# Second product of a feed-forward kernel: column halves of TensorE take two blocks of 512 tokens instead of two halves of one block's tokens, for the last 64 outputs

## The chip, the cores and the metric

The program runs on one core of one Trainium2 chip. The metric is the device time of one execution in microseconds. Times inside an execution come from a profiled run, and count from its first instruction.

## What is computed

A causal convolution with 7 taps, whose weights are a softmax made for each token and head, is followed by a feed-forward layer with a squared ReLU. There are 32,768 tokens of 192 numbers, and 2,048 hidden units.

```python
w = exp(weight_gen - max(weight_gen, -1)); w = w / (sum(w, -1) + 1e-9)   # 8 heads, 7 taps
x = einsum('bshk,bskhg->bshg', w, x_unf)       # x_unf: the last 7 tokens, 24 channels a head
h = x @ w_in                                   # 192 -> 2048
g = maximum(h, 0) ** 2
out = g @ w_out                                # 2048 -> 192
```

## The kernel before

**Tiling.** Each of the 128 partitions owns 256 consecutive tokens. A chunk is 4 tokens of every partition, 512 tokens; there are `NCH` = 64 chunks. VectorE makes the convolution of a later chunk (multiplies, line 344, and adds, line 349), the transposed result goes through DRAM and back (lines 525, 531, 536), and ScalarE and VectorE split it into a high and a low half-precision part (lines 392, 398). Every second chunk, the odd ones, also loads two chunks of input (`load_group`, lines 110 and 111) and works out their scales (`size_steps`, `descale`: line 138 on ScalarE, six small instructions on VectorE).

**Batches.** A chunk has 4 batches (b = 0 to 3) of two pairs j of feed-forward blocks. A block is 128 hidden units. In each batch TensorE does the first product of its own two pairs (`mm1`, line 565) and then the second product of the two pairs of the batch before (`mm2`), so the second product of a chunk's last batch falls into batch 0 of the next chunk. Meanwhile ScalarE takes each pair out of PSUM with `relu` (line 572), squares it (`square`, 576) and rounds it to half precision (`high`, 580); VectorE subtracts to get the remainder (`low`, 584). The order on every engine is the order in which the program is written, with `late` putting the `low`s of a batch into the next batch, after its first product, and `todo` the pieces of convolution behind them.

**TensorE in quarters.** The array works as four tiles of 64 rows by 64 columns. The row halves take the two halves of a block's 128 hidden units and write their sums to two PSUM banks; the column halves write to the lower and the upper 64 partitions. Products are made three times: high by high, high by low weights, low by high.

**The second product, transposed.** For chunks 4 to 62 (`turned(c)`, 59 chunks) outputs lie on partitions and tokens on columns. The first accumulator, `accs[c][0]`, takes outputs 0 to 127 (column halves: 0 to 63 and 64 to 127) with 512 tokens in each of two banks. The second, `accs[c][1]`, takes outputs 128 to 191; there the column halves are given two halves of 256 tokens each (line 617). There is one buffer of each accumulator.

**Taking it out.** In batch 1 of the next chunk, after that batch's first product is issued, `finish` copies one bank of each accumulator to SBUF with ScalarE (line 679) and adds the other bank with VectorE (line 680), 512 columns for the first and 256 for the second accumulator. The second product of the new chunk, which is next on TensorE, needs both accumulators free. Then `store_turned` scales the sums (line 702), transposes them (line 703) and issues 24 output DMAs on SyncE's queue (line 710).

Of the kernel before, what the change touches and what calls it, by code (L numbers as in the profile page):

```python
# [8 lines left out]
F32 = mybir.dt.float32  # L9
# [4 lines left out]
ALU = mybir.AluOpType  # L14
# [15 lines left out]
def kernel(  # L30
# [9 lines left out]
    nc = tc.nc  # L40
    B, S, D = x.shape
# [3 lines left out]
    P = 128  # L45
# [4 lines left out]
    TC = 4  # L50
    NCH = n_chunks or R // TC
# [3 lines left out]
    D1 = 64  # L55
    ND = D // D1
    N = TC * P
    NJ = NF // 2
# [12 lines left out]
    op = ctx.enter_context(tc.tile_pool(name="op", bufs=2))  # L71
# [13 lines left out]
    V = const.tile([P, NF, 3 * D], F16, name="V")  # L85
# [6 lines left out]
    act, ts, tt = nc.scalar.activation, nc.vector.tensor_scalar, nc.vector.tensor_tensor  # L92
# [69 lines left out]
    def descale(gi):  # L162
        row = att.tile([P, Q], F32, name="f", bufs=3)
        f = falls[gi] = row[:, 0:1]
        d = downs.pop(gi)
        dq = d.broadcast_to([P, Q])
        stt(out=row, in0=dq, scalar=back, in1=dq, op0=ALU.mult, op1=ALU.mult)
        if turned(gi * CPG):
            spread_falls[gi] = to_all(row)
# [23 lines left out]
    def block(j, i):  # L193
        return 4 * (j // 2) + 2 * i + j % 2
# [105 lines left out]
    HALVES = slice(0, D1), slice(D1, P)  # L300
# [240 lines left out]
    phs, rgs, ghs, gls, accs = {}, {}, {}, {}, {}  # L541

    def turned(c):
        return TURNED <= c < NCH - 1
# [33 lines left out]
    def high(c, j):  # L578
        gh = ghs[c, j] = gp.tile([P, 2, N], F16, name="gh")
        act(gh, rgs[c, j], AF.Copy, scale=1.0 / LIFT)  # L580
# [5 lines left out]
    def new_accs(c):  # L586
        accs[c] = [ps_o.tile([P, 2, N], F32, name=f"acc{i}") for i in range(2 if c else 1)]
# [14 lines left out]
    def mm2_turned(c, j):  # L602
        if j == 0:
            new_accs(c)
        gh, gl = ghs.pop((c, j)), gls.pop((c, j))
        for i in range(2):
            fb = block(j, i)
            for n, g in enumerate((gh, gh, gl)):
                fl = dict(start=fb == 0 and n == 0, stop=fb == NF - 1 and n == 2)
                for col in HALVES:  # L610
                    for r, rows in enumerate(HALVES):
                        d = n * D + col.start
                        nc.tensor.matmul(accs[c][0][col, r], V[rows, fb, d:d + D1], g[rows, i], **fl)  # L613
                for m, col in enumerate(HALVES):
                    for r, rows in enumerate(HALVES):
                        d = n * D + P
                        nc.tensor.matmul(  # L617
                            accs[c][1][col, r, 0:N // 2], V[rows, fb, d:d + D1],
                            g[rows, i, m * N // 2:(m + 1) * N // 2], **fl,
                        )  # L620

    ends = {}

# [40 lines left out]
    outs, sums_t = {}, {}  # L664

    def finish(c, p):
        if c == 0:
            if p == 0:
                outs[c] = op.tile([P, TC, D], F32, name="o_sb")
            nc.scalar.copy(outs[c][:, 2 * p:2 * p + 2], accs[c][0][:, :, p * D:(p + 1) * D])  # L670
            return
        acc = accs[c][p]
        if turned(c):
            if p == 0:
                sums_t[c] = op.tile([P, TC * D], F32, name="s", bufs=1)
            n0, n1 = ((0, N), (N, N + N // 2))[p]
            n = n1 - n0
            tmp = op.tile([P, N], F32, name="tmp")
            nc.scalar.copy(tmp[:, 0:n], acc[:, 1, 0:n])
            tt(out=sums_t[c][:, n0:n1], in0=acc[:, 0, 0:n], in1=tmp[:, 0:n], op=ALU.add)  # L680
            return
        if p == 0:
            outs[c] = op.tile([P, TC, D], F32, name="o_sb")
        o = outs[c][:, 2 * p:2 * p + 2]
        f = falls[c // CPG]
        o = o.rearrange("p t d -> p (t d)")
        tmp = op.tile([P, N], F32, name="tmp")
        n = 2 * D
        act(tmp[:, 0:n], acc[:, 1, 0:n], AF.Copy, scale=f)
        stt(out=o, in0=acc[:, 0, 0:n], scalar=f, in1=tmp[:, 0:n], op0=ALU.mult, op1=ALU.add)  # L690

    def finish_last(c):
        o = outs[c]
        for t in range(TC):
            stt(out=o[:, t], in0=ends[t], scalar=falls[c // CPG], in1=o[:, t], op0=ALU.mult, op1=ALU.add)
            nc.sync.dma_start(out=out_v[:, c * TC + t, :], in_=o[:, t])

    def store_turned(c):
        o = op.tile([P, TC * D], F32, name="o_sb")
        sm = sums_t.pop(c)  # L700
        sb = sm.rearrange("p (t n) -> p t n", n=P)
        tt(out=sb, in0=sb, in1=spread_falls[c // CPG].broadcast_to(sb.shape), op=ALU.mult)
        nc.vector.transpose(o, sm)  # L703
        for col in range(0, D, Q):
            for t in range(TC):
                if col < P:
                    p0, n0 = col, t * P
                else:
                    p0, n0 = 2 * t // TC * D1 + col - P, N + t % 2 * P
                nc.sync.dma_start(  # L710
                    out=out_v[:, c * TC + t, col:col + Q].rearrange("(q i) j -> i q j", i=Q),
                    in_=o[p0:p0 + Q, n0:n0 + P].rearrange("i (q j) -> i q j", j=Q),
                )

    def store(c):
        nc.sync.dma_start(out=out_v[:, c * TC:(c + 1) * TC, :], in_=outs[c])
# [112 lines left out]
    for p in range(2):  # L829
        finish(0, p)  # L830
# [14 lines left out]
    def at(c, b, f):  # L845
        todo.setdefault((c + b // NB, b % NB), []).append(f)
# [41 lines left out]
    for c in range(1, NCH + 1):  # L888
        for b in range(NB if c < NCH else 2):
            js = (2 * b, 2 * b + 1)  # L890
            if c < NCH:
                if b == 0 and c % 2 and (c + 3) // 2 * CPG < NCH:
                    load_group((c + 3) // 2)
                if c % 2 and b == 2 and (c + 3) // 2 * CPG < NCH:
                    total, scales = size_steps((c + 3) // 2)
                    b1 = 5 if c == 1 else 2
                    at(c, b1, total)
                    b2 = 6 if c == 1 else 3
                    at(c, b2, scales)
                    at(c, b2, lambda gi=(c + 3) // 2: descale(gi))  # L900
                if b == 0 and c + 2 < NCH and c + 2 > 2:
                    plan_conv(c + 2)
                for j in js:
                    mm1(c, j)
            early = b == 1 and 2 <= c <= TURNED
            if early:
                for p in range(2):
                    finish(c - 1, p)
            run(late)
            late.clear()  # L910
            if c == NCH and b == 1:
                finish_last(c - 1)
            elif b == (0 if c == NCH else 1) and c > 1:
                for p in range(0 if early else 2):
                    finish(c - 1, p)
                if turned(c - 1):
                    store_turned(c - 1)
                elif c < NCH:
                    store(c - 1)
            turn = turns.pop(c + 1, None) if b == NB - 1 else None  # L920
            if b == NB - 1 and c + 1 in splits and turn is None:
                for f in splits.pop(c + 1):
                    f()
            if pend and turn is None:
                mm2(*pend.pop(0))
            elif pend:
                one = pend.pop(0)
                mm2(*one, slice(0, 3))
                turn[0]()
                mm2(*one, slice(3, 4))  # L930
                turn[1]()
                mm2(*one, slice(4, 8))
            if c < NCH:
                relu(c, js[0])
                square(c, js[0])
                relu(c, js[1])
                high(c, js[0])
                sp = splits.pop(c + 1) if turn is not None else []
                run(sp[:1])
                square(c, js[1])  # L940
                run(sp[1:3])
                high(c, js[1])
                pend.append((c, b))
                late += [lambda c=c, j=js[0]: low(c, j)] + between.pop((c, b), [])
                late += [lambda c=c, j=js[1]: low(c, j)] + behind.pop((c, b), [])
                fs = todo.pop((c, b), [])
                if sp:
                    run(fs[:2])
                    run(sp[3:4])
                    run(fs[2:4])  # L950
                    run(sp[4:])
                    run(fs[4:])
                else:
                    run(fs)
# [30 lines left out]
```

## Time and profile before

| | us |
|---|---|
| median of 3 runs | 2036.22 |
| lowest, highest | 2035.5, 2037.34 |
| the profiled execution, first to last instruction (span) | 2033.1 |
| median less span | 3.1 |
| TensorE busy | 2024.1 (100%) |
| VectorE busy | 1864.3 (92%) |
| ScalarE busy | 1747.0 (86%) |

The profile gives the span of the execution, not its time with what lies around it; the difference to the median of the runs stands in the table in its place. In the rows PE is TensorE, PEld its weight loads, DVE is VectorE, ACT ScalarE, SPq SyncE's queue. A busy matmul engine is one that has a matmul in flight; four matmuls on four tiles run at once.

### The profile page before, as it was taken

Reading aid. Unit: us, or ns where it says so; the run is one execution under the profiler, and the core shown is the slowest. Engines: PE = TensorE matmul, PEld = TensorE weight load, DVE = VectorE, ACT = ScalarE, POOL = GpSimd, SP = SyncE. Lnnn points to the kernel's source line nnn. Section 1 sums busy time; section 2 is a strip of 40 time slices with the busy share of each in tenths; the row PEclk is TensorE's granted clock in tenths of the full one; section 3 lists DMA queues with packets and bytes.
Section 4 is the critical chain, followed back from the end, with each engine's and each line's share of the span. In section 5 each row is a group of like instructions: output and inputs, shape, how many; then the busy total and the mean of one; then the engine's idle time right before and its main releaser. Section 6 shows DMA issues by size and latency. Waiting matters only on the chain.

```text
span 2033.1 us, 92340 instructions
## 1 busy us (share of the span) xinstructions
PE 2024.1 (100%) x42124; PEld 1473.8 (72%) x42124; DVE 1864.3 (92%) x2457; ACT 1747.0 (86%) x2011; POOL 13.7 (1%) x18
## 2 busy tenths in 40 slices
PE   9999999999999999999999999999999999999999
PEld 8777777777777777777777777777777777777776
DVE  8999999999999999999999999999999999999984
ACT  6988888888888888888888888888888888888887
POOL 2000000000000000000000000000000000000000
PEclk9999999999999999999999999999999999999999
DMA  6233333332332333333323333333233233333321
GB/s 189 64 97 91 74 65 76 89 94 74 66 89 73 96 82 84 62 78 89 93 73 65 90 75 94 84 71 74 73 95 92 72 65 82 82 96 77 59 60 23
DMA packets 303552, 164.02 MB, mean 81 GB/s; under 512 B 215360, under 2 KB 273728, under 8 KB 299192
## 3 DMA queue, kind: packets, MB, share of 16 engines
q1 hardware_dynamic: 303160, 158.11, 32.0%
q8 instruction: 329, 5.39, 1.1%
q14 instruction: 63, 0.52, 0.1%
HBM read 108.43 MB, written 49.56 MB: 78 GB/s over the span
## 4 chain that ended last, share of the span: by engine, by line
PE 95%; DVE 3%; DMA 1%; ACT 0%; issue 0%; SPq 0%; POOL 0%; DVEq 0%
PE ph L565 47%; PE acc L613 30%; PE acc L617 15%; PE acc L658 1%; PE acc L597 1%; DVE pr L344 1%; DVE pr L349 1%; DVE gl L584 1%; DMA xT<-xd 0%; DMA xl<-xd 0%; DMA xd<-xr 0%; DMA wt<-in_weight_gen_dram 0%; DVE o_sb L690 0%; PE ph L633 0%; DMA xt<-in_x_dram 0%
## 5 line engine op out<-in xcount | busy, mean ns | idle before, releaser
L565 PEld LDWEIGHTS <-W 64*64 64x64 f16 (+1 forms) x17568 | 634.8, 107 | 319.5 <-issue 4.1
L565 PE MATMUL ph<-xh,W 64*64 64x512 f16 (+1 forms) x11712 | 754.6, 376 | 0.0
L572 ACT ACTIVATE g<-ph 128x1024 f32<-128x1024 f32 x504 | 512.0, 1016 | 239.4 <-PE ph L565 239.4
L584 DVE SCALAR_TENSOR_TENSOR gl<-gh,g 128x1024 f16<-128x1024 f16 x504 | 609.3, 1220 | 110.1 <-ACT gh L580 99.3
L613 PE MATMUL acc<-gh,V 64*64 64x512 f16 x7552 | 696.3, 376 | 0.0
L617 PE MATMUL acc<-gh,V 64*64 64x256 f16 x7552 | 576.9, 269 | 0.1
L613 PEld LDWEIGHTS <-V 64*64 64x64 f16 x11328 | 406.8, 107 | 205.6 <-issue 1.1
L576 ACT ACTIVATE g<-g 128x1024 f32<-128x1024 f32 x512 | 538.8, 1052 | 8.0
L580 ACT ACTIVATE gh<-g 128x1024 f16<-128x1024 f32 x504 | 530.2, 1052 | 8.0
L565 PE MATMUL ph<-xl,W 64*64 64x512 f16 (+1 forms) x5856 | 428.7, 376 | 1.5 <-DMA xl<-xd 1.1
L617 PEld LDWEIGHTS <-V 64*64 64x64 f16 x11328 | 406.7, 107 | 17.2 <-issue 0.3
L344 DVE TENSOR_TENSOR pr<-xt,wt 128x768 f32<-128x768 f32 x434 | 408.1, 953 | 2.1
L613 PE MATMUL acc<-gl,V 64*64 64x512 f16 x3776 | 389.4, 376 | 0.5 <-DVE gl L584 0.5
L349 DVE TENSOR_TENSOR pr<-pr 128x768 f32<-128x768 f32 x376 | 358.8, 954 | 2.2
L617 PE MATMUL acc<-gl,V 64*64 64x256 f16 x3776 | 288.4, 269 | 0.0
L398 DVE TENSOR_TENSOR xl<-xT,xh 128x512 f16<-128x512 f32 x180 | 113.6, 686 | 21.3 <-ACT xh L392 19.8
L392 ACT CAST xh<-xT 128x512 f16<-128x512 f32 x180 | 98.5, 610 | 0.9 <-DMA xT<-xd 0.9
L658 PE MATMUL acc<-V,gh 64*128 64x192 f16 x960 | 62.6, 243 | 0.0
L658 PE MATMUL acc<-V,gl 64*128 64x192 f16 x480 | 60.8, 243 | 0.1
L525 DVE STREAM_TRANSPOSE xr<-pr 128x768 f32<-128x768 f32 x60 | 58.7, 979 | 2.1
L680 DVE TENSOR_TENSOR s<-acc,tmp 128x512 f32<-128x512 f32 x118 | 59.9, 550 | 0.0
L703 DVE STREAM_TRANSPOSE o_sb<-s 128x768 f32<-128x768 f32 x59 | 57.7, 978 | 2.1
(99 smaller groups left out, 680.5 us busy)
## 6 DMA issues: line engine op xcount, KB each, us to landing
xT<-xd SPq DMA_DIRECT2D x120, 384.0 KB
xt<-in_x_dram SPq DMA_DIRECT2D x31, 1344.0 KB
xd<-xr SPq DMA_DIRECT2D x240, 96.0 KB
out_dram<-o_sb SPq DMA_DIRECT2D x1416, 16.0 KB
wt<-in_weight_gen_dram SPq DMA_DIRECT2D x31, 224.0 KB
raw<-in_moe_w_in_dram SPq DMA_DIRECT2D x8, 384.0 KB
raw<-in_moe_w_out_dram SPq DMA_DIRECT2D x4, 768.0 KB
fd<-ft SPq DMA_DIRECT2D x124, 0.1 KB
```

What stands on the lines that cost most here:

```text
L344: tt(out=dst, in0=src, in1=taps_w[0][:, :, k:k + 1].broadcast_to([P, n, G]), op=ALU.mult)
L349: on.tensor_tensor(out=prs[k0], in0=prs[k0], in1=prs.pop(k), op=ALU.add)
L392: nc.scalar.copy(xh, xs)
L398: tt(out=xl, in0=xs, in1=xh, op=ALU.subtract)
L565: nc.tensor.matmul(to, w[rows, k, j % 2, col], xs, **fl)
L572: act(r, phs.pop((c, j)), AF.Relu, scale=RHO * LIFT ** 0.5)
L576: act(r, r, AF.Square)
L580: act(gh, rgs[c, j], AF.Copy, scale=1.0 / LIFT)
L584: stt(out=gl, in0=ghs[c, j], scalar=-LIFT, in1=rgs.pop((c, j)), op0=ALU.mult, op1=ALU.add)
L613: nc.tensor.matmul(accs[c][0][col, r], V[rows, fb, d:d + D1], g[rows, i], **fl)
L617: nc.tensor.matmul(accs[c][1][col, r, 0:N // 2], V[rows, fb, d:d + D1], g[rows, i, m * N // 2:(m + 1) * N // 2], **fl,)
L658: nc.tensor.matmul(accs[c][t // 2][:, h, t % 2 * D:(t % 2 + 1) * D], g[rows, i, t * P:(t + 1) * P], V[rows, fb, n * D:(n + 1) * D], start= ...
```

## The change

For outputs 128 to 191 the two column halves no longer take two halves of the tokens of one block, but all 512 tokens of the two blocks of a pair: the lower 64 partitions sum over one block of each pair, the upper over the other. A pair and a product then have two groups of four 512-column matmuls for the first accumulator and one for the second, where they had two of 512 and two of 256 columns. The two partial sums on the two partition halves have to be added. `finish` now makes the second sum over all 512 columns into `thirds`; `swap_thirds`, on ScalarE in batch 1 between the first `high` and the second `square`, moves two blocks of 64 partitions by 256 columns to the other partition half; `add_thirds`, on VectorE in batch 2 after that batch's `low`s, adds them to what stands there. `store_turned` moves behind it, from batch 1 to batch 2.

```diff
+        fbs = [block(j, i) for i in range(2)]
+        for n, g in enumerate((gh, gh, gl)):
+            for i, fb in enumerate(fbs):
                 fl = dict(start=fb == 0 and n == 0, stop=fb == NF - 1 and n == 2)
                 for col in HALVES:
                     for r, rows in enumerate(HALVES):
                         d = n * D + col.start
                         nc.tensor.matmul(accs[c][0][col, r], V[rows, fb, d:d + D1], g[rows, i], **fl)
-                for m, col in enumerate(HALVES):
-                    for r, rows in enumerate(HALVES):
-                        d = n * D + P
-                        nc.tensor.matmul(
-                            accs[c][1][col, r, 0:N // 2], V[rows, fb, d:d + D1],
-                            g[rows, i, m * N // 2:(m + 1) * N // 2], **fl,
-                        )
+            fl = dict(start=j == 0 and n == 0, stop=j == NJ - 1 and n == 2)
+            for i, col in enumerate(HALVES):
+                for r, rows in enumerate(HALVES):
+                    d = n * D + P
+                    nc.tensor.matmul(accs[c][1][col, r], V[rows, fbs[i], d:d + D1], g[rows, i], **fl)
...
         if turned(c):
+            tmp = op.tile([P, N], F32, name="tmp")
+            nc.scalar.copy(tmp, acc[:, 1])
             if p == 0:
-                sums_t[c] = op.tile([P, TC * D], F32, name="s", bufs=1)
-            n0, n1 = ((0, N), (N, N + N // 2))[p]
-            n = n1 - n0
-            tmp = op.tile([P, N], F32, name="tmp")
-            nc.scalar.copy(tmp[:, 0:n], acc[:, 1, 0:n])
-            tt(out=sums_t[c][:, n0:n1], in0=acc[:, 0, 0:n], in1=tmp[:, 0:n], op=ALU.add)
+                to = sums_t[c] = op.tile([P, TC * D], F32, name="s", bufs=1)
+            else:
+                to = thirds[c] = tmp
+            tt(out=to[:, 0:N], in0=acc[:, 0], in1=tmp, op=ALU.add)
             return
...
+    def swap_thirds(c):
+        sw = thirds[c, "other"] = op.tile([P, N // 2], F32, name="sw", bufs=1)
+        for m, rows in enumerate(HALVES):
+            nc.scalar.copy(sw[rows], thirds[c][HALVES[1 - m], m * N // 2:(m + 1) * N // 2])
+
+    def add_thirds(c):
+        t, sw = thirds.pop(c), thirds.pop((c, "other"))
+        for m, rows in enumerate(HALVES):
+            tt(out=sums_t[c][rows, N:], in0=t[rows, m * N // 2:(m + 1) * N // 2], in1=sw[rows], op=ALU.add)
...
-                if turned(c - 1):
-                    store_turned(c - 1)
-                elif c < NCH:
+                if c < NCH and not turned(c - 1):
                     store(c - 1)
+            if b == 2 and c < NCH and turned(c - 1):
+                add_thirds(c - 1)
+                store_turned(c - 1)
...
                 high(c, js[0])
+                if b == 1 and turned(c - 1):
+                    swap_thirds(c - 1)
                 sp = splits.pop(c + 1) if turn is not None else []
                 run(sp[:1])
                 square(c, js[1])
```

## Rows read from the trace of the kernel before

**Rows 1.** The page: span, busy us (share) of each engine, the chain by engine.

```profile
span 2033.1 us, 92340 instructions
...
PE 2024.1 (100%) x42124; PEld 1473.8 (72%) x42124; DVE 1864.3 (92%) x2457; ACT 1747.0 (86%) x2011; POOL 13.7 (1%) x18
...
PE 95%; DVE 3%; DMA 1%; ACT 0%; issue 0%; SPq 0%; POOL 0%; DVEq 0%
```

**Rows 2.** Timeline, TensorE, one batch: start us, us, instructions, [idle before].

```profile
1036.55 1.49 PE L565 MATMUL ph<-xh,W 64*64 64x512 f16 x24
...
1040.43 0.41 PE L613 MATMUL acc<-gh,V 64*64 64x512 f16 x4
...
1044.33 0.41 PE L565 MATMUL ph<-xh,W 64*64 64x512 f16 x4
```

**Rows 3.** Timeline, VectorE: the adds in batch 1 of chunks 6 and 60.

```profile
229.41 1.01 DVE L680 TENSOR_TENSOR s<-acc,tmp 128x512 f32<-128x512 f32 x2
...
1910.96 1.02 DVE L680 TENSOR_TENSOR s<-acc,tmp 128x512 f32<-128x512 f32 x2
```

**Rows 4.** Timeline, VectorE, from batch 1 of an odd chunk to that of the next.

```profile
1008.04 0.96 DVE L702 TENSOR_TENSOR s<-s,fs 128x768 f32<-128x768 f32 x1
...
1009.93 0.34 DVE L329 TENSOR_REDUCE sm<-wt 128x32 f32<-128x224 f32 x1
...
1012.28 2.58 DVE L584 SCALAR_TENSOR_TENSOR gl<-gh,g 128x1024 f16<-128x1024 f16 x2
...
1019.38 1.23 DVE L584 SCALAR_TENSOR_TENSOR gl<-gh,g 128x1024 f16<-128x1024 f16 x1 [0.17 <-ACT gh L580]
1021.42 1.23 DVE L584 SCALAR_TENSOR_TENSOR gl<-gh,g 128x1024 f16<-128x1024 f16 x1 [0.81 <-ACT gh L580]
1023.39 1.90 DVE L398 TENSOR_TENSOR xl<-xT,xh 128x512 f16<-128x512 f32 x3 [0.75 <-ACT xh L392]
...
1027.81 0.15 DVE L142 TENSOR_TENSOR down<-a 128x1 f32<-128x1 f32 x1
...
1028.98 1.18 DVE L584 SCALAR_TENSOR_TENSOR gl<-gh,g 128x1024 f16<-128x1024 f16 x1
1030.33 1.23 DVE L584 SCALAR_TENSOR_TENSOR gl<-gh,g 128x1024 f16<-128x1024 f16 x1 [0.16 <-ACT gh L580]
...
1036.46 0.39 DVE L327 TENSOR_TENSOR wt<-wt,mx 128x224 f32<-128x224 f32 x1
...
1039.04 1.02 DVE L680 TENSOR_TENSOR s<-acc,tmp 128x512 f32<-128x512 f32 x2
```

**Rows 5.** Timeline, ScalarE, batch 1 of the odd and of the next chunk.

```profile
1012.55 1.06 ACT L580 ACTIVATE gh<-g 128x1024 f16<-128x1024 f32 x1
1015.38 1.03 ACT L572 ACTIVATE g<-ph 128x1024 f32<-128x1024 f32 x1 [1.77 <-PE ph L565]
...
1036.89 0.39 ACT L328 ACTIVATE wt<-wt 128x224 f32<-128x224 f32 x1
...
1038.73 1.02 ACT L572 ACTIVATE g<-ph 128x1024 f32<-128x1024 f32 x1 [0.70 <-PE ph L565]
```

**Rows 6.** One line's instructions: ns min/median/max, first and last start, forms.

```profile
L383 ACT COPY xT<-ph x4: 356/366/369, 17.8 to 18.9; 64x256 f32<-64x256 f32 x4
...
L680 DVE TENSOR_TENSOR s<-acc,tmp x118: 412/550/686, 197.4 to 2004.2; 128x512 f32<-128x512 f32 x59, 128x256 f32<-128x256 f32 x59
```

**Rows 7.** Timelines, ScalarE and VectorE, prologue: one 128x512 and two 64x512 each.

```profile
88.32 1.78 ACT L462 CAST xh<-ph 128x512 f16<-128x512 f32 x3
...
90.13 2.11 DVE L468 TENSOR_TENSOR xl<-ph,xh 128x512 f16<-128x512 f32 x3 [1.34 <-ACT xh L462]
```

**Rows 8.** Timeline, SyncE's queue: start us, us over which it issued.

```profile
1010.04 14.81 SPq L710 DMA_DIRECT2D out_dram<-o_sb  x24
...
1055.63 0.43 SPq L110 DMA_DIRECT2D wt<-in_weight_gen_dram  x1
```

**Rows 9.** Windows, a load's 6 us: busy us by engine, TensorE's clock, DMA share, GB/s.

```profile
995.00:1001.00 6.00, 6.00 (x136) 4.34 (x132) 5.08 (x7) 4.16 (x6) 0.00 (x0) 1.00 0.75 273
```

More of the change, by code (lines that the diff above doesn't have):

```diff
@@ L605, in mm2_turned @@
         gh, gl = ghs.pop((c, j)), gls.pop((c, j))
-        for i in range(2):
-            fb = block(j, i)
-            for n, g in enumerate((gh, gh, gl)):
+        fbs = [block(j, i) for i in range(2)]
+        for n, g in enumerate((gh, gh, gl)):
+            for i, fb in enumerate(fbs):
                 fl = dict(start=fb == 0 and n == 0, stop=fb == NF - 1 and n == 2)
@@ L690, in finish @@
         stt(out=o, in0=acc[:, 0, 0:n], scalar=f, in1=tmp[:, 0:n], op0=ALU.mult, op1=ALU.add)
+    thirds = {}
+    def swap_thirds(c):
[6 more added lines that the diff above has]
+            tt(out=sums_t[c][rows, N:], in0=t[rows, m * N // 2:(m + 1) * N // 2], in1=sw[rows], op=ALU.add)
     def finish_last(c):
```

## The prediction

> **What bounds the kernel now.** I read the page's busy times and the chain of work that ended last first [rows 1]. TensorE is busy for 100% of the span and 95% of the chain is matmuls; VectorE stands at 92% and ScalarE at 86%. So the matmul stream sets the time, and VectorE has some 8% to spare. Next I read TensorE's timeline of the steady state [rows 2]: a batch is one block of the first product (72 matmuls, 1036.55 to 1040.43, 3.88 us) and one of the second (1040.43 to 1044.33, 3.90 us), with nothing between them. Four batches make a chunk. The two late pairs of VectorE adds shown lie 54 chunks apart [rows 3]: (1910.96 - 229.41) / 54 = 31.14 us a chunk, 7.785 a batch, so 3.885 and 3.900 for the two blocks. Turned chunks are 59 of the 64.
>
> Then come VectorE's and ScalarE's timelines [rows 4, 5]. They repeat every two chunks, since an odd chunk also prepares the scales of the next load. Call O an odd chunk's batch 1, beginning at 1005.40, and E the next chunk's, at 1036.55. The reader should look at how late VectorE adds the two accumulators of the chunk before. In O both adds are done before 1008.04, and TensorE asks for the accumulators at 1009.29, one chunk ahead of 1040.43; in E they run from 1039.04 to 1040.06, and TensorE asks at 1040.43 [rows 2, 4]. 0.37 us is all the cover there is, every second chunk. Both ends of the run have this late pair [rows 3].
>
> **The matmuls.** A second-product block has 12 groups of four 512-column matmuls and 12 groups of four 256-column ones; it gets 18 groups of 512 instead. The columns streamed are the same. The first product's block is 18 groups of 512 in 3.885 us, 0.2158 a group; a pair of 512 and 256 takes 3.900 / 12 = 0.3250, so the 256 takes 0.1092. Two sizes give 0.1066 us for 256 columns and 2.6 ns that belong to a group whatever its size. New block: 3.885, so 15 ns less. 59 chunks x 4 blocks x 0.015 = 3.5 us. That the four matmuls of a new group read four different streams costs nothing: the 256-column groups already do. The four weight loads that go with each dropped group ran beside matmuls.
>
> A rule speaks of this same term. The rows give 2.6 ns for a group's fixed part. The Trainium skill, page TensorEngine Tiling (Array Packing), section Instruction Overhead, gives about 60 cycles to each matmul; an estimate from it, at 2.4 GHz, is 25 ns for each of the 59 x 24 = 1,416 groups dropped, 35 us in place of 3.5. The trace disagrees with that for matmuls in a packed stream, and I keep 3.5.
>
> **ScalarE.** The second copy out of the accumulators grows from 256 to 512 columns; even a whole 512-column cast (0.59 [rows 7]) fits into the 0.70 us for which ScalarE then waits for TensorE [rows 5]. New are two copies of 64x256 in batch 1, between the first `high` and the second `square`. They delay the second `high`, which ends at 1013.61 (1012.55 + 1.06), by a. ScalarE's next batch doesn't suffer: it waits 1.77 us there [rows 5]. VectorE does, since its second `low` of this batch starts when that `high` ends, 0.03 later. Price of a: the 64x256 copies of the prologue take 0.366 each [rows 6], and three casts of 512 columns in a row, two of them on 64 partitions, take 1.78, 0.59 apiece [rows 7]. Two adds on all partitions overlap by 0.08 (0.69 and 0.41 together take 1.02 [rows 4, 6]); if the copies did too, they would cost 2 x 0.285 = 0.57, and if they are as dear as 512 columns 1.2. The casts on 64 partitions are the nearest in kind and show hardly any overlap, so I take 2 x 0.39, and 0.07 for an overlap lost at the border: a = 0.85.
>
> **VectorE.** Its second add grows from 256 to 512 columns (0.41 to 0.69 [rows 6]). Two adds of 64x256 are new, t together. They and the scaling and transpose of `store_turned` (1008.04 to 1009.93, 1.89 us [rows 4]) go from batch 1 to batch 2, behind the two `low`s. Price of t: 224 columns in SBUF take 0.39 [rows 4], 0.31 with overlap; three subtractions of 512 columns, two of them on 64 partitions, take 2.11, 0.70 each [rows 7]. So from 0.62 to 1.4. 256 columns fewer are 0.27 less (0.69 against 0.41 [rows 6]), which makes 0.43 each without overlap, and 0.09 for an overlap lost at the border: t = 0.95.
>
> **Where that lands.** Batch 1 becomes light for VectorE and can't keep what it saves: the second `low` can't start before 13.64 + a on the clock of this stretch (1000 left off), so VectorE stands idle ahead of it. From there to the adds in E it has, before, 39.04 - 13.64 = 25.40 us, in which it waits 0.17, 0.81, 0.75 and 0.16, and loses some 0.08 of overlap at each wait; 23.2 is work [rows 4]. Once it runs late those waits vanish. After: 13.64 + a + 23.2 + t + 1.89 brings it to the first add, and the two adds take 0.60 + 0.68. The second accumulator is free at 40.01 + a + t. TensorE, 4 x 0.015 sooner at that block, first writes it after two groups of 512: 40.43 - 0.06 + 0.43 = 40.80. The stall is s - 0.79 with s = a + t. At s = 1.80 it is 1.01 us, most of it ahead of the first group, since the first accumulator is late as well.
>
> In an even chunk the way is shorter by the six small scale instructions (1027.81 to 1028.98, 1.2 us [rows 4]). But ScalarE's `exp` now waits for VectorE's late subtraction (it starts at 1036.89, the subtraction ends at 1036.85 [rows 4, 5]); this shifts the first `relu` of E by s - 0.88, and with it the `high` that VectorE's second `low` waits for. Written out as above, the even chunk would stall by s - 2.08 (TensorE is already s - 0.79 later): none at 1.80.
>
> The other waits for VectorE are covered. Batch 2's first `low`, at 1019.38 before [rows 4], starts at 13.64 + a + 1.14 + t + 1.89 + 4.35 (five multiplies and adds) = 22.8 and ends 1.2 later. TensorE reads it at 9.29 + 2 x 7.785 + 1.30 = 26.2, since the new order comes to `gl` after six groups of 0.216 (0.65 us before). 2 us of cover, here and in batch 3; were it gone, the lateness would go straight into the block.
>
> So one stall in each pair: E is chunk 6, 8, ... 60, 28 of them. 28 x 1.01 = 28.3 us lost, 3.5 won, +24.8.
>
> **Moved queues.** The 24 output DMAs of a chunk take SyncE's queue 14.81 us [rows 8]. They start some 8.6 us later (L703 ends at 18.6 instead of 10.0). Behind them stand the scale row's small DMAs, wanted two chunks on, the turn of the next chunk, itself 1 us later, and every second time the loads, issued at 1055.6 before [rows 8] and about 1064.2 after. The 6 us in which the loads before them ran moved 1.6 MB (273 GB/s [rows 9]), and ScalarE first reads a load in batch 2 of the odd chunk that follows, which begins at 1036.55 + 31.14 + 7.79 = 1075.5. 11 us of cover for 6; cost zero. Were it gone, ScalarE would wait, in order, ahead of its casts, and each us beyond it would cost TensorE up to a us for each of some 30 loads.
>
> **Rivals.** First, the queues hide it all: VectorE has 8% to spare, and the two engines' added work, 1.8 us in 31.14, is less than that. For it: the shares [rows 1]. Against: the spare time sits ahead of the second `low`, where it can't be saved up. It decides at s below 0.79, yet the cheapest prices give 0.57 + 0.62 = 1.19. Time: 2036.2 - 3.5 = 2032.7. Chance 0.10.
>
> Second, both chunks of a pair stall, from s = 2.08, if 64 partitions cost far more than I priced. At s = 2.3: 1.51 + 0.22, 28 times, 48.4 - 3.5: 2081. Against: it needs prices near those of 512 columns. Chance 0.08.
>
> Third, a dropped group is worth more than 2.6 ns, and the stall stays. To end level it would have to be (28.3 - 3.5) / 1,416 = 17.5 ns more; at 30 ns in all the time is 2061 - 1,416 x 0.0274 = 2022. Against it stand the two group sizes, which fix the number [rows 2]. Chance 0.02. This is the mechanism of the rule on overhead above; by the 25 ns of that page the time would be 2061 - 32 = 2029.
>
> **The numbers.** The profiled execution's span is 2033.1; the median of the runs is 3.1 more, and I take that for what lies around the span. 2033.1 + 24.8 = 2057.9, and 2061 us. The likeliest case (0.80) alone runs from s = 1.19 (0.40 x 28 - 3.5, 2044) to s = 2.08 (1.29 x 28 - 3.5, 2069). For 8 in 10 I leave the first and third rival out below and go a little into the second above, to s = 2.2 (1.41 + 0.12, 28 times): 2044 to 2076. About 0.2%, 4 us, is what can be told from no change: slower 0.87 (nearly all of the likeliest, and the second), same 0.09 (most of the first, a little of the likeliest), faster 0.04 (the third and the edge of the first).
>
> **What would show it.** Second-product blocks of 3.885 us without a wait inside. In every even chunk's batch 1 TensorE idle for about 1 us ahead of its first group on the accumulators, released by the VectorE add; none in odd ones. 64x256 copies that start 0.39 apart and adds 0.45 apart; the second `low` about 9.1 us behind the block's start in O, with idle ahead of it; the waits of 0.81 and 0.75 gone. The prediction is wrong if VectorE makes up the time between (s below 0.79), or if TensorE waits elsewhere: for `gl`, or for the turned input.

## The result, and the profile after

The changed kernel takes 2060.98 us (median of 4 runs, 2060.13 to 2061.27) against 2036.18 for the kernel before (4 runs beside it): a ratio of 1.0122, 95% interval 1.011 to 1.0134. It is slower by 24.8 us. The profiled execution took 2060.13, with a span of 2058.4; the span is 25.3 longer than before [rows 1].

The page of the changed kernel: span, busy time of each engine, and the chain that ended last by engine.

```profile
span 2058.4 us, 81103 instructions
...
PE 2031.0 (99%) x36460; PEld 1369.5 (67%) x36460; DVE 1905.5 (93%) x2575; ACT 1815.4 (88%) x2129; POOL 13.0 (1%) x18
...
PE 51%; DVE 32%; ACT 9%; DMA 3%; SPq 2%; issue 2%; DVEq 0%; POOL 0%
```

VectorE's share rises by one point only, from 92% to 93%, and ScalarE's by two [rows 1]. But the chain, which was matmuls for 95% of the span, is now matmuls for 51% and VectorE for 32%: at some points TensorE waits, and the way back from there leads through VectorE's queue. The waits of the changed kernel say where (total us, times, longest):

```profile
PE acc L613 <- DVE s L678: 19.0, 28, 1.0
```

It happens 28 times, each time on the adds that empty the accumulators. TensorE's timeline of the changed kernel shows a pair of chunks: batch 1 of an odd chunk (O, at 1016.83) and that of the even one behind it (E, at 1047.91), up to the next O.

```profile
1016.83 1.49 PE L565 MATMUL ph<-xh,W 64*64 64x512 f16 x24
...
1020.71 0.63 PE L613 MATMUL acc<-gh,V 64*64 64x512 f16 x8
1021.14 0.41 PE L618 MATMUL acc<-gh,V 64*64 64x512 f16 x4
...
1047.91 1.49 PE L565 MATMUL ph<-xh,W 64*64 64x512 f16 x24
...
1051.14 0.84 PE L565 MATMUL ph<-xl,W 64*64 64x512 f16 x12
1052.65 0.63 PE L613 MATMUL acc<-gh,V 64*64 64x512 f16 x8 [0.67 <-DVE s L678]
1053.25 0.41 PE L618 MATMUL acc<-gh,V 64*64 64x512 f16 x4
...
1080.01 1.49 PE L565 MATMUL ph<-xh,W 64*64 64x512 f16 x24
```

In O the second product starts 3.88 us behind the start of the first, without a wait. In E it starts 4.74 us behind it, 0.86 late, and its first group on the second accumulator is another 0.17 late (0.60 behind the first in place of 0.43). So O to E takes 31.08 us and E to the next O 32.10. Before, a chunk took 31.14 [rows 3]. The 0.67 in brackets is less than the delay, since the row counts the last matmul of the first product as in flight until 1051.98.

ScalarE's timeline of the changed kernel in O, from the first `high` to the second:

```profile
1021.93 1.05 ACT L580 ACTIVATE gh<-g 128x1024 f16<-128x1024 f32 x1
1023.01 0.82 ACT L695 COPY sw<-tmp 64x256 f32<-64x256 f32 x2
1023.85 1.06 ACT L576 ACTIVATE g<-g 128x1024 f32<-128x1024 f32 x1
1024.94 1.06 ACT L580 ACTIVATE gh<-g 128x1024 f16<-128x1024 f32 x1
```

The second `high` ends at 1026.00, 9.17 us into O; it was 8.21 before (1013.61 - 1005.40 [rows 2, 5]). So a is 0.96. VectorE's timeline of the changed kernel, from there to the accumulators in E:

```profile
1026.03 1.23 DVE L584 SCALAR_TENSOR_TENSOR gl<-gh,g 128x1024 f16<-128x1024 f16 x1 [1.64 <-ACT gh L580]
1027.17 0.84 DVE L700 TENSOR_TENSOR s<-tmp,sw 64x256 f32<-64x256 f32 x2
1028.05 0.96 DVE L712 TENSOR_TENSOR s<-s,fs 128x768 f32<-128x768 f32 x1
1029.04 0.98 DVE L713 STREAM_TRANSPOSE o_sb<-s 128x768 f32<-128x768 f32 x1
...
1034.25 2.35 DVE L584 SCALAR_TENSOR_TENSOR gl<-gh,g 128x1024 f16<-128x1024 f16 x2
1036.52 1.89 DVE L398 TENSOR_TENSOR xl<-xT,xh 128x512 f16<-128x512 f32 x3
...
1049.65 2.35 DVE L584 SCALAR_TENSOR_TENSOR gl<-gh,g 128x1024 f16<-128x1024 f16 x2
1051.91 0.68 DVE L678 TENSOR_TENSOR s<-acc,tmp 128x512 f32<-128x512 f32 x1
1052.52 0.68 DVE L678 TENSOR_TENSOR tmp<-acc,tmp 128x512 f32<-128x512 f32 x1
```

VectorE stands idle for 1.64 us ahead of the second `low`, and from there it works without a pause: the waits of 0.81 and 0.75 that it had in the next batch before [rows 4] are gone, the two `low`s there run as one piece of 2.35. Still the adds come 4.00 us into E, where they came 2.49 into it before (1039.04 - 1036.55 [rows 2, 4]). The two new adds delay the scaling by 0.88 (1027.17 to 1028.05): this is t. So s is 1.84.

The sum over the run: 28 x 1.02 = 28.6 lost, 59 chunks x 0.06 = 3.5 won, 25.1 more; the span grew by 25.3. (By the lengths of the chunks 27 of the 28 stalls are 1.02 to 1.04 and one, late in the run, is 1.37.)

### The profile page after: what moved, and what is told of

It reads as the page before. It is cut to its first block, busy times and chain, and to the rows that moved or that the text cites. A ratio compares the mean times of both kernels' runs of the same rounds, so it can differ in the third digit from the quotient of the medians.

```text
span 2058.4 us, 81103 instructions
## 1 busy us (share of the span) xinstructions
PE 2031.0 (99%) x36460; PEld 1369.5 (67%) x36460; DVE 1905.5 (93%) x2575; ACT 1815.4 (88%) x2129; POOL 13.0 (1%) x18
## 4 chain that ended last, share of the span: by engine, by line
PE 51%; DVE 32%; ACT 9%; DMA 3%; SPq 2%; issue 2%; DVEq 0%; POOL 0%
PE ph L565 24%; PE acc L613 16%; DVE gl L584 10%; PE acc L618 8%; DVE pr L349 6%; DVE pr L344 6%; ACT g L576 3%; ACT gh L580 3%; ACT g L572 3%; DVE xl L398 2%; SPq L720 2%; DVE xr L525 1%; DMA fs<-fd 1%; DVE o_sb L713 1%; DVE s L712 1%
## 5 line engine op out<-in xcount | busy, mean ns | idle before, releaser
L565 PEld LDWEIGHTS <-W 64*64 64x64 f16 (+1 forms) x17568 | 645.8, 107 | 334.0 <-issue 4.6
L584 DVE SCALAR_TENSOR_TENSOR gl<-gh,g 128x1024 f16<-128x1024 f16 x504 | 598.5, 1218 | 114.2 <-ACT gh L580 113.7
L613 PE MATMUL acc<-gh,V 64*64 64x512 f16 x7552 | 593.7, 376 | 19.0 <-DVE s L678 19.0
L613 PEld LDWEIGHTS <-V 64*64 64x64 f16 x11328 | 406.7, 107 | 226.9 <-issue 28.4
L618 PE MATMUL acc<-gh,V 64*64 64x512 f16 x3776 | 390.0, 377 | 0.0
L613 PE MATMUL acc<-gl,V 64*64 64x512 f16 x3776 | 296.9, 376 | 0.1
L618 PEld LDWEIGHTS <-V 64*64 64x64 f16 x5664 | 206.3, 107 | 109.6 <-issue 8.0
L618 PE MATMUL acc<-gl,V 64*64 64x512 f16 x1888 | 195.0, 376 | 0.0
L328 ACT ACTIVATE wt<-wt 128x224 f32<-128x224 f32 x64 | 24.9, 389 | 52.7 <-DVE wt L327 49.5
L673 ACT COPY tmp<-acc 128x512 f32<-128x512 f32 x118 | 62.1, 578 | 0.0
```

The source lines that it names most:

```text
L565: nc.tensor.matmul(to, w[rows, k, j % 2, col], xs, **fl)
L584: stt(out=gl, in0=ghs[c, j], scalar=-LIFT, in1=rgs.pop((c, j)), op0=ALU.mult, op1=ALU.add)
L618: nc.tensor.matmul(accs[c][1][col, r], V[rows, fbs[i], d:d + D1], g[rows, i], **fl)
```

## The experiments

Each edit is made in the changed kernel. The runs of the kernel before that stand beside them have medians of 2035.85 (groups alone, no half sum, copies later, adds first) and 2036.08 (the other four), 27 runs each; the spans compare with 2033.1 before [rows 1]. "Stall" is what a chunk takes from one batch 1 to the next over the 31.08 us in which TensorE doesn't wait.

### The matmuls alone

```diff
 # finish: 256 columns for the second accumulator, as before
-            tmp = op.tile([P, N], F32, name="tmp")
-            nc.scalar.copy(tmp, acc[:, 1])
...
+            n0, n1 = ((0, N), (N, N + N // 2))[p]
+            n = n1 - n0
+            tmp = op.tile([P, N], F32, name="tmp")
+            nc.scalar.copy(tmp[:, 0:n], acc[:, 1, 0:n])
+            tt(out=sums_t[c][:, n0:n1], in0=acc[:, 0, 0:n], in1=tmp[:, 0:n], op=ALU.add)
...
+                if turned(c - 1):
+                    store_turned(c - 1)
...
-                add_thirds(c - 1)
-                store_turned(c - 1)
...
-                    swap_thirds(c - 1)
```

> Only the new matmul groups; the second accumulator is taken out as before (256 columns, store in batch 1), no copies to the other half, no added sums, so the sum over the partition halves is left out. Theory (a late VectorE add stalls TensorE by s - 0.79 in every even chunk; the groups save 15 ns a block): no stall, 2036.2 - 3.5 = 2032.7 us, second-product blocks of 3.885 us. Rival A (a dropped group is worth far more than 2.6 ns): 2010 us or less. Rival B (the new groups cost time themselves, part of the 25 us): above 2037 us.

Measured: 2032.08 us, ratio 0.9979 (0.997 to 0.9988), span 2030.2. Every chunk of the steady state takes 31.08. The regrouping is worth 3.8 us (2.4 to 6.1 by the interval), which is 2.7 ns for each of the 1,416 groups dropped (1.7 to 4.3). The second product's block is now as long as the first's. TensorE's timeline of this kernel, one batch:

```profile
942.31 1.49 PE L565 MATMUL ph<-xh,W 64*64 64x512 f16 x24
...
946.19 0.63 PE L613 MATMUL acc<-gh,V 64*64 64x512 f16 x8
...
950.08 1.49 PE L565 MATMUL ph<-xh,W 64*64 64x512 f16 x24
```

The blocks take 3.88 and 3.89 us. The third rival of the prediction, a group worth tens of ns, falls, and so does rival B: new groups that cost time would have shown here. The Trainium skill, page TensorEngine Tiling (Array Packing), section Instruction Overhead, gives about 60 cycles to each matmul, by an estimate 25 ns a group at 2.4 GHz; in this packed stream a tenth of that was measured.

### Everything but the copies and the adds

```diff
-                    swap_thirds(c - 1)
...
-                add_thirds(c - 1)
```

The 512-column adds of `finish` stay, and so does the place of `store_turned` in batch 2. What the cut above leaves out: the second add now writes into a wider tile of sums, of which `store_turned` takes the first 768 columns.

> The changed kernel without the two copies and the two adds (the sum over the partition halves is left out); 512-column add and the store in batch 2 stay. Theory: s = 0, no stall, 2032.7 us. Rival C (the store's move to batch 2, with its scaling, transpose and 24 DMAs, is what delays): stays near 2061 us, or at least above 2045.

Measured: 2031.96 us, ratio 0.9979 (0.997 to 0.9987), span 2030.3, all chunks 31.08. TensorE's timeline of this kernel, two chunks' batch 1:

```profile
911.27 1.49 PE L565 MATMUL ph<-xh,W 64*64 64x512 f16 x24
...
942.35 1.49 PE L565 MATMUL ph<-xh,W 64*64 64x512 f16 x24
```

With s at zero there is no stall. The store's move and that of its 24 DMAs, the wider copy and the wider add cost nothing that can be measured, so rival C falls.

### The copies without the adds

```diff
 # swap_thirds writes to the place of the sum
-        sw = thirds[c, "other"] = op.tile([P, N // 2], F32, name="sw", bufs=1)
...
-            nc.scalar.copy(sw[rows], thirds[c][HALVES[1 - m], m * N // 2:(m + 1) * N // 2])
+            nc.scalar.copy(sums_t[c][rows, N:], thirds[c][HALVES[1 - m], m * N // 2:(m + 1) * N // 2])
...
-                add_thirds(c - 1)
+                thirds.pop(c - 1)
```

> The changed kernel with the two copies but without the two added sums: the copies write over the last 64 outputs' sums, so half of the partial sums is left out. t = 0, s = a = 0.96. Theory: a stall of 0.15 us in 28 chunks, 4.2 us, against 3.8 won: 2036 us, and the second low of odd chunks still 9.2 us into batch 1. Rival H (ScalarE's copies are what stalls TensorE, the adds are beside the point): near 2061.

Measured: 2035.84 us, ratio 0.9998 (0.9989 to 1.0008), span 2034.5. TensorE's timeline of this kernel, the first blocks of batch 1 in an odd chunk, an even one and the next odd one:

```profile
881.84 1.49 PE L565 MATMUL ph<-xh,W 64*64 64x512 f16 x24
...
912.92 1.49 PE L565 MATMUL ph<-xh,W 64*64 64x512 f16 x24
...
944.13 1.49 PE L565 MATMUL ph<-xh,W 64*64 64x512 f16 x24
```

31.08, then 31.21: a stall of 0.13 in the even chunk for s = 0.96, where the sum gives 0.96 - 0.79 = 0.17; the second `low` starts 9.19 into the odd one, as in the changed kernel. All of the copies' delay but this is swallowed, and rival H falls; from here to the changed kernel s grows by 0.88 and the stall by 0.89.

### The copies twice over

```diff
-        for m, rows in enumerate(HALVES):
+        for m, rows in list(enumerate(HALVES)) * 2:
             nc.scalar.copy(sw[rows], thirds[c][HALVES[1 - m], m * N // 2:(m + 1) * N // 2])
```

> The changed kernel with each of the two copies to the other partition half made twice. ScalarE's part a goes from 0.96 to 1.80 and s from 1.84 to 2.68. Theory: even chunks' batch 1 stalls by s - 0.81 = 1.87 us, and now the odd ones too, by s - 2.08 = 0.60: 28 x 2.47 = 69 less 3.8 won, some 2101 us. Rival F (the stall is a fixed wait, not the excess over a slack): 2036 + 28 x (1.03 + 0.84) - 4, 2084 us, with stalls in even chunks alone. Rival G (ScalarE has room and only VectorE's work counts): stays near 2061.

Measured: 2100.04 us, ratio 1.0314 (1.03 to 1.0328), span 2098.2. TensorE's timeline of this kernel, an odd, an even and the next odd chunk's batch 1 (the last row is cut by the window):

```profile
905.99 1.49 PE L565 MATMUL ph<-xh,W 64*64 64x512 f16 x24
...
937.70 1.49 PE L565 MATMUL ph<-xh,W 64*64 64x512 f16 x24
...
970.54 0.62 PE L565 MATMUL ph<-xh,W 64*64 64x512 f16 x6
```

And the waits of this kernel:

```profile
PE acc L613 <- DVE s L678: 47.3, 56, 1.7
```

ScalarE's timeline of this kernel, in the odd chunk of the rows above:

```profile
907.45 0.39 ACT L328 ACTIVATE wt<-wt 128x224 f32<-128x224 f32 x1 [1.03 <-DVE wt L327]
...
915.46 1.06 ACT L580 ACTIVATE gh<-g 128x1024 f16<-128x1024 f32 x1
```

Now both chunks of a pair stall, 56 times in all, as the second rival of the prediction has it; rival F, with stalls in even chunks alone, and rival G fall. Four copies take 1.67 in place of 0.82, so s is 0.85 more, 2.69. The odd chunk stalls by 31.71 - 31.08 = 0.63 (the sum gives 2.69 - 2.08 = 0.61), the even one by 32.84 - 31.08 = 1.76 (the sum gives 1.90). The 0.14 between come from the odd chunk: `exp` (L328) waits 1.03 there for VectorE's late subtraction, so the second `high` ends 10.53 into it instead of 9.17 + 0.85 = 10.02, 0.51 later, while TensorE is itself 0.63 later by the stall of that chunk. 1.90 + 0.51 - 0.63 = 1.78.

### The copies behind the second `high`

```diff
                 high(c, js[0])
-                if b == 1 and turned(c - 1):
-                    swap_thirds(c - 1)
...
                 high(c, js[1])
+                if b == 1 and turned(c - 1):
+                    swap_thirds(c - 1)
```

> The changed kernel with the two copies behind the second high of batch 1 instead of ahead of the second square. Same work on every engine. Theory: a = 0, s = t = 0.88, a stall of some 0.07 us in 28 chunks, 2 us: 2034 to 2036 us; the second low starts 8.2 us into batch 1, as before the change. Rival D (the added load of ScalarE and VectorE as such is the cost): stays near 2061 us.

Measured: 2034.24 us, ratio 0.9992 (0.9983 to 1.0), span 2032.5. Timelines of this kernel in an odd chunk: the start of its batch 1 on TensorE, then ScalarE, then VectorE:

```profile
942.88 1.49 PE L565 MATMUL ph<-xh,W 64*64 64x512 f16 x24
...
951.09 0.83 ACT L695 COPY sw<-tmp 64x256 f32<-64x256 f32 x2
952.83 1.03 ACT L572 ACTIVATE g<-ph 128x1024 f32<-128x1024 f32 x1 [0.91 <-PE ph L565]
...
951.10 1.22 DVE L584 SCALAR_TENSOR_TENSOR gl<-gh,g 128x1024 f16<-128x1024 f16 x1 [0.81 <-ACT gh L580]
952.24 0.86 DVE L700 TENSOR_TENSOR s<-tmp,sw 64x256 f32<-64x256 f32 x2
953.14 0.96 DVE L712 TENSOR_TENSOR s<-s,fs 128x768 f32<-128x768 f32 x1
```

The copies now lie in the time in which ScalarE waits for TensorE, and it still waits for 0.91. The second `low` starts 8.22 into the odd chunk, as before (8.24 = 1013.64 - 1005.40); s is t alone, 0.90 here (952.24 to 953.14), and the stall 0.08. Rival D falls: all of the added work is still there. By the spans, this move of two instructions wins back 25.9 us (2058.4 less 2032.5).

### And half of the scaling earlier

```diff
 # added to "the copies behind the second high"
+    def scale_first(c):
+        sb = sums_t[c][:, 0:N].rearrange("p (t n) -> p t n", n=P)
+        tt(out=sb, in0=sb, in1=spread_falls[c // CPG].broadcast_to(sb.shape), op=ALU.mult)
...
 # store_turned: only the last 256 columns
+        sb = sb[:, TC:]
...
-                if c < NCH and not turned(c - 1):
+                if turned(c - 1):
+                    scale_first(c - 1)
+                elif c < NCH:
                     store(c - 1)
```

> Copies behind the second high, and the scaling of the first 512 columns in batch 1, where VectorE stands idle; only the last 256 are scaled in batch 2. Theory: the chain to the adds of even chunks gets 0.5 us shorter, which takes away the 0.08 us that is left with the copies moved: no stall, 2032.1 us, a chunk pair of 62.16 us. If something else makes up the 2.2 us between that run and the groups alone: 2034 us again.

Measured: 2031.63 us, ratio 0.9978 (0.9969 to 0.9987), span 2030.4, all chunks 31.08. VectorE's timeline of this kernel in an odd chunk, the two parts of the scaling:

```profile
945.28 0.68 DVE L710 TENSOR_TENSOR s<-s,fs 128x512 f32<-128x512 f32 x1
...
952.74 0.42 DVE L717 TENSOR_TENSOR s<-s,fs 128x256 f32<-128x256 f32 x1
```

The stall is gone with all of the change's work kept: 512 columns are scaled in batch 1, where VectorE stood idle, and what stands behind the second `low` takes 0.42 instead of 0.96.

### The accumulators first

```diff
-            early = b == 1 and 2 <= c <= TURNED
+            early = b == 1 and 2 <= c < NCH
```

With `early`, so far used in chunks 2 to 4 alone, `finish` runs ahead of the `low`s of the batch before on VectorE's queue.

> The changed kernel with the two adds out of the accumulators ahead of the two lows in batch 1, in every chunk. Same work. Theory: the accumulators come free 2.3 us sooner, which is more than the stall of 1.03; the lows have 1.3 us of the block before they are read. No stall, 2032.7 us. Rival D: stays near 2061 us. Rival E (the lows are then late and TensorE waits for gl): above 2040 us, with waits of the gl matmuls.

Measured: 2051.43 us, ratio 1.0076 (1.0063 to 1.0088), span 2049.7: a miss by 19 us. ScalarE's timeline of this kernel in an even chunk:

```profile
1046.55 0.39 ACT L328 ACTIVATE wt<-wt 128x224 f32<-128x224 f32 x1 [2.11 <-DVE wt L327]
1046.84 1.06 ACT L673 COPY tmp<-acc 128x512 f32<-128x512 f32 x2
```

And VectorE's:

```profile
1046.12 0.39 DVE L327 TENSOR_TENSOR wt<-wt,mx 128x224 f32<-128x224 f32 x1
1047.44 0.69 DVE L678 TENSOR_TENSOR s<-acc,tmp 128x512 f32<-128x512 f32 x1 [0.93 <-ACT tmp L673]
```

`exp` (L328) stands in ScalarE's queue ahead of the copies out of the accumulators and waits 2.11 us for VectorE's late subtraction (L327). VectorE does that subtraction and then waits 0.93 for the copies that `exp` held up. TensorE's timeline of this kernel in that chunk shows what is left:

```profile
1044.02 1.49 PE L565 MATMUL ph<-xh,W 64*64 64x512 f16 x24
...
1048.19 0.63 PE L613 MATMUL acc<-gh,V 64*64 64x512 f16 x8
...
1049.92 0.63 PE L613 MATMUL acc<-gl,V 64*64 64x512 f16 x8
```

The stall shrinks to 0.71 a pair. The second product starts 4.17 us behind the start of the first in place of 3.88, and its first groups on `gl` start 1.73 behind that in place of 1.30: 0.17 of this is the second accumulator, the rest the `low`s, which stand behind the late adds. So rival E holds in part. The prediction had named this wait of `exp`; the expectation overlooked it.

### The accumulators first, and `exp` behind their copies

```diff
 # added to "the accumulators first"
-        for f in a[:3]:
+        for f in a[:3] if m == N_PE + 1 else a[:2]:
             at(m - 2, 2 * int(m == N_PE + 1), f)
+        if m > N_PE + 1:
+            exps[m - 2] = a[2]
...
             if early:
                 for p in range(2):
                     finish(c - 1, p)
+                run([exps.pop(c)] if c in exps else [])
```

> The adds ahead of the lows, as tried, and ScalarE's exp behind the two copies out of the accumulators instead of ahead of them. Theory of the miss: the copies stood behind an exp that waits for VectorE's late subtraction, so that VectorE waited 0.93 us for them. With the exp behind them VectorE doesn't wait, the accumulators are free 3.8 us into batch 1: no stall or under 0.1 us, 2032 to 2035 us. If the lows are what is late instead: above 2045 us, with TensorE's waits on gl.

Measured: 2031.16 us, ratio 0.9976 (0.9967 to 0.9985), span 2029.3, all chunks 31.08. ScalarE's timeline of this kernel in an even chunk:

```profile
910.44 1.05 ACT L673 COPY tmp<-acc 128x512 f32<-128x512 f32 x2
911.96 0.39 ACT L328 ACTIVATE wt<-wt 128x224 f32<-128x224 f32 x1 [0.47 <-DVE wt L327]
```

And VectorE's:

```profile
911.54 0.39 DVE L327 TENSOR_TENSOR wt<-wt,mx 128x224 f32<-128x224 f32 x1
911.85 0.68 DVE L678 TENSOR_TENSOR s<-acc,tmp 128x512 f32<-128x512 f32 x1
```

The copies no longer stand behind `exp`, and the adds follow the subtraction at once. This holds the whole change, with the copies where the change put them, and is faster than both kernels: by 4.9 us than before, and by some 30 than the changed kernel. It can't be told from the split scaling (2031.63): both have no stall left and only the dropped groups to show.

## Why the prediction was right

**The mechanism.** A stall of s less a slack of 0.79 in each even chunk, none in the odd one, was the likeliest case, and it is what happened, 28 times. The change was forecast at 24.8 us and is 24.8 by the medians, 25.3 by the spans. That the time, 2061.0, was met to 0.02 is luck: the 3.1 us taken for what lies around the span are 1.7 to 1.8 in the four executions of the changed kernel, and their spans, 2058.4 (the profiled one) to 2059.5, are longer than the 2057.9 of the forecast; the two errors cancel. The experiments move s and the stall follows: without copies and adds none, 0.08 at s = 0.90, 0.13 at 0.96, 1.02 at 1.84, 1.76 at 2.69, where the odd chunk joins in with 0.63. The slack that the first three of these stalls give is 0.82 to 0.83, where 0.79 was worked out. The adds, with the copies out of the way, cost 0.08, and the copies alone 0.13, together 1.02. That is the signature of a slack used up, and it speaks against any story in which one of the two is the culprit.

**The two sizes.** a was 0.96, not 0.85, and t 0.88, not 0.95; the errors nearly cancel (1.84 against 1.80), which is luck. One line's instructions in the changed kernel (ns min/median/max, first and last start, form):

```profile
L695 ACT COPY sw<-tmp x118: 402/403/407, 201.6 to 2034.1; 64x256 f32<-64x256 f32 x118
...
L700 DVE TENSOR_TENSOR s<-tmp,sw x118: 407/417/424, 205.7 to 2038.2; 64x256 f32<-64x256 f32 x118
```

The copy takes 0.403, more than the 0.366 of the same form out of PSUM [rows 6], and two take 0.82 in place of 0.78. The rest of a, 0.14, is lost at the borders, where 0.07 was allowed: before, the square started 0.10 ahead of the end of the first `high` (1011.47 against 1010.52 + 1.05); now the copies start 0.03 after the `high` ahead of them has ended, and the square starts 0.02 after they have. The adds were priced at 0.43 and take 0.417, and of the 0.09 allowed for borders little was lost, since the first starts 0.09 before the end of the `low` ahead of it (1027.26).

**The dropped groups.** 3.5 us forecast; 3.8 measured on their own, 3.5 by the chunk's length (31.14 to 31.08).

**What was costed at nothing.** The store's move: its last step ends 13.19 us into O, where 13.2 was worked out (18.6 less 5.40), and without the half sum the move costs nothing. The `low`s of batch 2 start 17.42 us into O, where 17.4 was worked out, and delay no matmul. The loads are issued 27.1 us into E (1075.04 less 1047.91), where 27.7 was worked out (1064.2 less 1036.55), and no wait for a load appears in the steady state. The margin of 11 us for the loads was not tried further.

**The rivals.** That the queues hide it all fails as argued: 7% of VectorE's span is still idle in the changed kernel, and 1.64 us of it stand in each pair ahead of the second `low`, where the order of this program has no work for them; the split scaling shows that work moved there can use them. The odd chunk's stall fits the threshold of s = 2.08 that was worked out: none at 1.84, 0.63 at 2.69, where 0.61 was expected. No run lies nearer to it.

**Where a step went wrong** was not in the prediction but in an expectation behind it: that adds put first are free of the delay. They are, once what stands ahead of their copies on ScalarE is moved too.

## What to carry to other kernels

An engine's idle share says little about added work: find the last wait that it can't avoid before the point at which the bounding engine asks, add up its queue from there, and compare with the cover that is left; here some 0.8 us was free, and each us beyond it, paid in 28 pairs of chunks, cost 28. Here small copies did best behind the instruction for which another engine waited, and the emptying of an accumulator ahead of work that could wait, once what stood ahead of it on the other engine was moved too: look at the order on every engine. When two added pieces each look free alone, try them together.

## What was not expected of the hardware

In these kernels ScalarE's instructions on 64 partitions overlap less with their neighbours than those on 128 do. The 64x256 copies take 0.403 each, two 0.82 and four 1.67, and the instructions before and behind stand 0.02 to 0.03 off; elsewhere the same engine starts a 128x1024 instruction some 0.1 before the end of the one ahead, and two copies of 128x512, 0.578 each, take 1.05. The prologue's four copies of 64x256, 0.366 each, take 1.51, so they don't overlap either. On VectorE two 64x256 adds of 0.417 take 0.84, while two adds of 128x512 start 0.61 apart at 0.68 each; ahead of the first 64x256 add an overlap of 0.09 stays. (The scaling behind them reads what they write and stands 0.04 off, as it did before the change.) Whether it is the number of partitions, or the step from one partition half to the other between two such instructions, was not tried apart. The copy within SBUF is 0.037 dearer than the prologue's copy of the same form out of PSUM [rows 6]; whether that is the source or the crossing to the other partition half was not tried.
